# A linear-attention and gated-MLP block: a smaller mask build, other start-up loads, numerators at a 64-column stride and a new written-out order

## The chip, the cores and the metric

The kernel runs on one core of one Trainium2 chip. The core has five engines that run side by side, each with its own queue of instructions: TensorE (PE, matmuls, with its weight loads shown apart as PEld), VectorE (DVE), ScalarE (ACT), GpSimd (POOL) and SyncE (SP, which here only issues DMAs). They wait for each other by semaphores. Each engine executes in the order of its queue, so an instruction that waits holds up all that is queued behind it on that engine.

The metric is the device time of one execution in microseconds, as a median of several executions. The kernel before takes 272.32 us (three executions, 272.31 to 272.6).

## The reference

One transformer block, on 2048 rows of 640 columns in bf16. The attention is linear: 32 heads of 20 columns, with a feature map of two softmaxes.

```python
qkv = x_normed @ wqkv                        # q, k, v: 32 heads of 20
pq, pk = q @ w_phi[h], k @ w_phi[h]          # per head, 20 x 20
phi_q = concat(softmax(pq), softmax(-pq))    # 40 features per head; phi_k alike
kv  = phi_k^T v                              # per head, 40 x 20
z   = sum over rows of phi_k                 # per head, 40
o   = (phi_q kv) / (phi_q z + 1e-6)
h   = x + o @ wo                             # x_normed is layernorm(x)
h2  = h + ((n @ w_gate) * (n @ w_up)) @ w_down   # n is layernorm(h)
```

## The kernel before

The rows are cut in 16 tiles of 128 (t = 0 to 15), the 640 columns in 5 chunks of 128. Since q and k are used only behind w_phi, the kernel first multiplies the weights: Wk times the block-diagonal matrix of w_phi, and the same for Wq. After that each tile goes through these steps, which the code names by a letter and the tile:

- `x`: load; `L1s`, `L1a`: mean and variance on VectorE; `L1l`, `L1e`: reciprocal root by a logarithm and an exponential on ScalarE, for groups of tiles (`LNG`); `L1n`: minus mean times root, the shift that ScalarE needs to form the normalized row; `xn`: the normalized row; `xt`: its transpose, by a DMA, or on TensorE (tiles in `TPE`) with a copy out of PSUM, `xte`.
- `K`, `V`, `Q`: the three products, ten matmuls of about 320 columns each. For tiles 0 and 1 they are cut in five pieces of two (`TSPLIT`). `Ve` copies V out of PSUM; `Kx` and `Qx` take the exponentials of plus and minus, `Ks` and `Qs` the sums, `Kr`, `Ke`, `Qr`, `Qb`, `Qe` the reciprocals, and `Kn` and `Qn` multiply by them, on GpSimd. `KV`: eleven small matmuls, summed over the tiles in two PSUM banks. `qT`: the query features are transposed by a DMA.
- After all 16 `KV` the sums are masked to the heads (`KVe0`, `KVe1`). `N`: the numerators and denominators of a tile, eleven matmuls of 63 columns (three heads of 20 columns and a denominator). `dd`, `rd`, `o` on VectorE: denominator plus epsilon, reciprocal, product. `oT`: a DMA transposes `o`; `O`: the output product; `h`: the residual sum; `hc`: the centred row; `L2q`, `L2v`, `L2r`: the second variance; `hT`: a DMA transposes the row.
- `U`: gate and up products for blocks of 256 or 512 rows (`FB`), `g` and `u` multiply them, `D` is the down product, `y` adds it to the residual, `w` stores the tile. The last tile's D is cut in three pieces of columns (`LASTCUT`).

At the start stand, in addition: `warm`, products of zeros that keep TensorE busy until the loads are there (`NWARM`, `zero` makes their operand); `id0`, `id1`: the identity matrix for TensorE's transposes; `gl0`, `gla`, `glb`: a mask of heads, GL, by selects on GpSimd; `w5` loads w_phi and `Ph` multiplies it by the mask; `wk0` to `wk4` load Wk, `WT` transposes a chunk of it on TensorE, `WTe` copies it out, `F1` multiplies the chunk by the masked w_phi and `Fe1` copies the result. `wqt` and `F0`, `Fe0` do the same for Wq, later. So the path to the first product is: load of wk, WT, WTe, F1, Fe1, K; and beside it: load of x, L1s, L1a, L1l, L1e, xn, xt, xte, K. `K3` is the first product behind those of tiles 0 and 1.

The order is not the program's: every operation has an entry in the table `PLAN`, `name:key:alternative:banks`. The key is its place: `arrange` (L694) sorts all operations by it and gives each engine its queue. The alternative picks one of the engines that the operation allows (`alts`). The banks are its places in PSUM (eight banks of 2 KB per partition) or in a rotating buffer; whoever takes a place waits for the last user of the one before. So a wait for a free bank is decided by the table too. `emit` puts in the semaphores.

Of the kernel before, what the change touches and what calls it, by code (L numbers as in the profile page):

```python
# [8 lines left out]
ALU = mybir.AluOpType  # L9
# [23 lines left out]

NB = 11
# [17 lines left out]
id1:5.17 WT2:5.52::0 WTe2:6.139 WT0:5.958::1 WTe0:6.724 xt1:6.375::2 xt0:6.654::3 xte0:7.309 F1_2:6.933::4 WT1:7.252::6 WTe1:7.894:1 wk3:3.66 WT3:7.669::7
L1s2:6.426 Fe1_2:7.45 WTe3:8.289 xte1:8.697:1 F1_0:8.086::0 Fe1_0:8.603:1 wk4:4.14:1 WT4:8.405::3 WTe4:9.104:1 F1_1:8.822::4 Fe1_1:9.339 x3:4.62:1 x6:5.1
L1s3:9.512 L1a2:10.3 F1_3:9.141::6 Fe1_3:9.923 va1:5.414 L1a3:10.422 K0_0:9.46::0 L1s6:10.531 F1_4:9.731::2 Fe1_4:10.507:1 L1s7:11.319 wv0:5.58:1 V0_0:10.1::4
wv1:6.06 L1l2:11.091 x4:6.54 K0_1:10.371 K0_2:10.642 L1e2:11.417 L1s5:12.105 ekz:6.244 L1n2:11.697 V1_0:10.913::6 V1_1:11.184 L1n3:11.921 xn3:12.223:1:2
L1s4:12.893 L1a4:13.803 L1a7:13.912 K1_0:11.455::2 x12:7.02 wv2:7.5:1 K1_1:11.726 K0_3:11.997 wv4:7.98:1 L1a5:14.021 xn2:14.13::3 K1_2:12.268 K1_3:12.539
K1_4:12.81 V0_1:13.081 Kx1_0:13.28::0 Kx1_1:13.864 V1_2:13.352 wv3:8.46 wu1:8.94 L1a6:14.642 wg4:9.42 V0_2:13.623 V0_3:13.894 V0_4:14.165 wqt4:9.9 Ve0:14.635::0
V1_3:14.436 xt3:14.707::2 xte3:15.184:1 L1l4:15.219 L1e4:15.545 L1n5:15.825 K0_4:14.986 x8:11.21 Kx0_0:15.638::1 Kx0_1:16.222 Ks1:15.592::0 L1n4:16.049
V1_4:15.257 xt2:15.528::3 K3:15.807::4 Ve1:16.806::1 L1n7:16.985:1 L1n6:16.273 xn6:17.39:1:0 Kr1:18.195 V3:17.163::0 Ke1:18.486 Kn1:18.82 xn4:18.632:1:1
xn7:19.437:1:2 x10:11.69 wqt0:12.17 Ve3:20.242::2 xn5:17.16::3 xt5:17.785 rqz:21.133 xte2:17.672:1 L1s9:18.081 L1s11:18.867 Kx3_0:20.826::2 Kx3_1:21.41  # L60
Ks0:19.654::1 Kr0:21.994 K2:18.519::6 Kx2_0:22.14::3 Kx2_1:22.724 wqt2:19.096 Ke0:23.308 L1a9:21.047 V2:19.875::2 L1a11:21.157 L1s10:21.265 L1s8:22.052
L1a8:22.962 L1a10:23.072 L1l8:23.454 xt7:20.405 K5:21.231::0 Kx5_0:23.636::4 Ve2:23.18:1:3 xt4:21.715 L1e8:24.22 L1n10:24.5 V5:22.587::4 Ks3:23.912::2
Kx5_1:24.313 Ks5:25.305::3 L1n9:24.724 Ks2:26.698::0 x14:23.026 xn9:28.09::3 xt6:23.506 V7:23.943::6 Ve5:24.897::4 V4:25.299::2 L1n8:24.948 xn8:25.481:1:2
K4:26.655::0 Kn0:25.172 wqt3:24.816 Kr3:26.286 KV0:28.011::4,5 KV1:28.344 L1n11:28.602:1 L1s14:28.777 Ve7:26.432::5 Ke3:27.016 wqt1:26.125 xn10:27.162:1:1
Ve4:27.967::6 V6:28.677::6 Kr2:28.551 Kn3:27.485 Ke2:28.842 xn11:29.564::0 L1s12:30.076 Kx4_0:28.988::1 Kx4_1:29.572 Kn2:29.798 Kr5:30.156 Ve6:30.302::7
Ks4:30.863::1 xt8:27.436 xt9:28.745 L1s13:32.257 L1a13:33.166 K6:30.033::2 F0_1:31.389::0 xt11:30.189 K7:31.708::6 Fe0_1:31.906 wg2:31.5 wg3:31.98 L1a12:33.276
Kx6_0:32.49::0 KV2:33.064 KV3:33.397 Kr4:33.074 Kx6_1:33.22 Ke4:33.804 Kn4:34.138 F0_3:33.73::0 Fe0_3:34.247:1 Sz:36.451 L1a14:34.987 wu0:32.459 V8:34.049::2
# [151 lines left out]
def pool_c(n):  # L219
    return 0.183 + 0.0017 * n  # L220
# [692 lines left out]
```

## Time and profile before

| | |
|---|---|
| median of three executions | 272.32 us |
| profiled execution, its own time | 272.55 us |
| its span, first to last instruction | 270.8 us |
| PE busy | 266.0 us, 98% |
| DVE busy | 161.6 us, 60% |
| ACT busy | 123.8 us, 46% |
| POOL busy | 72.8 us, 27% |
| DMA | 27.76 MB, q1 47.3% of 16 engines, q10 1.6% |
| granted TensorE clock | 1.000 |

Busy time is the union of an engine's instructions; matmuls overlap each other, so the sum of the lengths shown is more than the time they take. The idle time in front of an instruction stands in square brackets with what ended it. The chain of waits follows the work back from the last instruction, each step to what released it. A load's time to landing counts from its issue. q1 is the queue of SP's DMAs, q10 that of ScalarE's.

### The profile page before, as it was taken

What the parts mean: (1) busy time and instruction counts of PE and PEld (TensorE: products, weight loads), DVE (VectorE), ACT (ScalarE), POOL (GpSimd) and SP (SyncE); (2) the same over time, 40 slices, a digit from 0 to 9 for tenths busy, and PEclk for the clock granted to TensorE, in tenths of its full rate; (3) what the DMA queues carried; (4) which work ended last, traced back from release to release, by engine and by line L of the source; (5) the groups of instructions that cost most, each with busy time, mean ns of one, the idle gap of its engine ahead of it and who ended that gap; (6) DMA issues with size and microseconds to landing.
All of it is one profiled execution on the core that took longest, in us unless ns stands there. A gap on an engine that the chain in (4) does not pass through costs nothing.

```text
span 270.8 us, 5184 instructions
## 1 busy us (share of the span) xinstructions
PE 266.0 (98%) x2103; PEld 177.1 (65%) x2103; DVE 161.6 (60%) x295; ACT 123.8 (46%) x304; POOL 72.8 (27%) x98
## 2 busy tenths in 40 slices
PE   7999999999999999999999999999999999999996
PEld 3877787777777689865656747775445457544774
DVE  4989999989689978887754434223123312424224
ACT  3999999788846667232254443003213510032000
POOL 8124989999942222331000000000000000000000
DMA  6997899967947989589347032041000000100003
GB/s 185 323 249 159 128 299 329 146 140 134 196 91 149 131 180 157 62 167 120 59 91 105 0 73 51 0 69 30 29 0 15 0 0 27 69 5 1 2 24 104
DMA packets 66600, 27.76 MB, mean 103 GB/s; under 512 B 57744, under 2 KB 65296, under 8 KB 66576
## 3 DMA queue, kind: packets, MB, share of 16 engines
q1 hardware_dynamic: 65120, 26.42, 47.3%
q10 hardware_dynamic: 1456, 1.01, 1.6%
q8 instruction: 16, 0.26, 0.4%
q14 instruction: 8, 0.07, 0.1%
HBM read 11.00 MB, written 2.62 MB: 50 GB/s over the span
## 4 chain that ended last, share of the span: by engine, by line
PE 90%; DVE 3%; DMA 3%; ACT 2%; POOL 1%; issue 0%; SPq 0%; DVEq 0%; POOLq 0%
PE ps L652 38%; PE ps L476 22%; PE ps L671 19%; PE ps L609 6%; PE ps L520 2%; DMA scratch<-ph 2%; PE ps L582 1%; DVE o L599 1%; PE ps L405 1%; DMA w<-in_A_w_phi_dram 1%; DVE sm L596 1%; ACT scratch L245 1%; POOL Phi L374 1%; DVE S L550 1%; ACT ph L545 0%; ACT ek L626 0%
## 5 line engine op out<-in xcount | busy, mean ns | idle before, releaser
L652 PE MATMUL ps<-xnT,Wgu 128*128 128x512 bf16 (+1 forms) x600 | 107.0, 336 | 0.0
L652 PEld LDWEIGHTS ps<-xnT,Wgu 128*128 128x128 bf16 x600 | 58.1, 98 | 43.4 <-DVE ev L660 0.4
L657 ACT ACTIVATE gt<-ps 128x512 bf16<-128x512 f32 (+1 forms) x60 | 29.0, 510 | 94.2 <-PE ps L652 90.4
L476 PE MATMUL ps<-Wp,xnT 128*128 128x320 bf16 (+1 forms) x480 | 68.8, 299 | 0.3 <-DVE o L599 0.2
L660 DVE TENSOR_TENSOR ev<-ps,gt 128x512 bf16<-128x512 f32 (+1 forms) x60 | 33.3, 580 | 41.7 <-PE ps L652 28.8
L476 PEld LDWEIGHTS ps<-Wp,xnT 128*128 128x128 bf16 x480 | 45.5, 97 | 18.3 <-DVE o L599 0.7
L671 PE MATMUL ps<-Wd,ev 128*128 128x320 bf16 (+2 forms) x396 | 53.3, 295 | 0.0
L671 PEld LDWEIGHTS ps<-Wd,ev 128*128 128x128 bf16 x396 | 38.1, 98 | 14.8
L512 POOL TENSOR_TENSOR ek<-ek,SR 128x1280 bf16<-128x1280 bf16 x16 | 37.5, 2357 | 4.0 <-ACT SR L497 3.9
L683 DVE SCALAR_TENSOR_TENSOR Wp<-ps,rs,x_all 128x640 bf16<-128x640 f32 (+3 forms) x18 | 14.4, 807 | 38.2 <-PE ps L671 38.1
L550 DVE TENSOR_REDUCE S<-ph 128x66 f32<-128x1320 bf16 x16 | 24.0, 1521 | 3.5 <-ACT ph L547 3.4
L630 POOL TENSOR_SCALAR ln<-mv 128x1 f32<-128x1 f32 x8 | 1.5, 190 | 89.3 <-ACT ek L626 88.9
L492 DVE TENSOR_REDUCE SR<-ek 128x64 f32<-128x1280 bf16 x16 | 23.3, 1478 | 1.2 <-ACT ek L488 1.0
L609 PE MATMUL ps<-Wo,Wp 128*128 128x320 bf16 x160 | 24.0, 299 | 0.0
L564 POOL TENSOR_TENSOR ph<-ph,RQ 128x660 bf16<-128x660 bf16 x16 | 20.8, 1306 | 10.2 <-ACT RQ L560 10.0
L545 ACT ACTIVATE ph<-ps 128x600 bf16<-128x600 f32 x32 | 21.2, 679 | 4.3 <-PE ps L476 3.6
L488 ACT ACTIVATE ek<-ps 128x640 bf16<-128x640 f32 x32 | 21.1, 701 | 0.5 <-PE ps L476 0.5
L609 PEld LDWEIGHTS ps<-Wo,Wp 128*128 128x128 bf16 x160 | 15.4, 98 | 6.7
L615 DVE SCALAR_TENSOR_TENSOR x_all<-ps,x_all 128x640 bf16<-128x640 f32 x16 | 13.1, 820 | 9.3 <-PE ps L609 9.2
L599 DVE TENSOR_TENSOR o<-ps,sm 128x720 bf16<-128x720 f32 x16 | 14.4, 903 | 1.3 <-DVE sm L596 0.5
L626 ACT ACTIVATE ek<-x_all,mv 128x640 bf16<-128x640 bf16 x16 | 13.1, 821 | 2.8 <-DVE x_all L615 2.8
L624 ACT ACTIVATE xn<-x_all,mv 128x640 bf16<-128x640 bf16 x10 | 8.2, 825 | 9.5 <-DVE x_all L615 9.5
(64 smaller groups left out, 166.3 us busy)
## 6 DMA issues: line engine op xcount, KB each, us to landing
out_dram<-Wp SPq DMA_DIRECT2D x15, 160.0 KB, 1.9
x_all<-in_A_x_dram SPq DMA_DIRECT2D x6, 320.0 KB, 6.1
Wgu<-in_B_w_up_dram SPq DMA_DIRECT2D x5, 384.0 KB, 6.4
Wgu<-in_B_w_gate_dram SPq DMA_DIRECT2D x5, 384.0 KB, 4.1
Wd<-in_B_w_down_dram SPq DMA_DIRECT2D x2, 480.0 KB, 6.8
Wd<-in_B_w_down_dram ACTq DMA_DIRECT2D x2, 480.0 KB, 4.5
ev<-in_A_wqkv_dram SPq DMA_DIRECT2D x5, 160.0 KB, 3.8
Wp<-in_A_wqkv_dram SPq DMA_DIRECT2D x5, 160.0 KB, 5.9
```

The lines of the kernel that those rows point to most:

```text
L476: ins = e.matmul(pb(b, hb)[:, 0:n1 - n0], lhsT=T["xnT"][:, NC - 1 - c, P * t:P * (t + 1)], rhs=T["Wp"][:, POS[kind], c, n0:n1], start=(c = ...
L488: G.op("act", "%sx%d_%d" % (nm, t, s), lambda e, s=s, b=b, ek=ek: e.activation(out=T["ek"][:, ek.slots[0], 0:2 * D].rearrange("p (b h s f) ...
L492: G.op("dve", "%ss%d" % (nm, t), lambda e, ek=ek, sr=sr: e.tensor_reduce(out=T["SR"][:, sr.slots[0], 0, :], in_=T["ek"][:, ek.slots[0], 0: ...
L512: G.op("pool", "Kn%d" % t, lambda e, eng, ek=ek, sr=sr: e.tensor_tensor(out=T["ek"][:, ek.slots[0], 0:2 * D].rearrange("p (h f) -> p h f", ...
L545: e.activation(out=v[:, 0:10].rearrange("p (b g) j f -> p b g j f", b=2), in_=pp(b, 0, 300).rearrange("p b (g j f) -> p b g j f", j=3, f=D ...
L550: G.op("dve", "Qs%d" % t, lambda e, t=t, ph=ph: e.tensor_reduce(out=T["S"][:, t, 0:66].rearrange("p (g k) -> p g k", k=6), in_=pv(ph).rear ...
L564: return e.tensor_tensor(out=v, in0=v, in1=T["RQ"][:, rq.slots[0], 1, 0:33].rearrange("p (g j) -> p g j", j=3).unsqueeze(3).to_broadcast([ ...
L609: ins = e.matmul(pb(b, hb)[:, 0:320], lhsT=T["oT"][:, oT.slots[0], c, :], rhs=T["Wo"][:, c, 320 * hb:320 * (hb + 1)], start=(c == 0), stop ...
L652: ins = e.matmul(pb(b)[:, 0:n], lhsT=T["Wgu"][:, gu, c, P * ft:P * (ft + 1)], rhs=T["xnT"][:, NC - 1 - c, o0:o0 + n], start=(c == 0), stop ...
L657: G.op("act", "g%d_%d" % (bi, ft), lambda e, pg=pg, gt=gt, n=n: e.activation(out=T["gt"][:, gt.slots[0], 0:n], in_=pb(pg)[:, 0:n], func=AF ...
L660: o_ = G.op("dve", "u%d_%d" % (bi, ft), lambda e, pu=pu, gt=gt, hh=hh, ft=ft, n=n: e.tensor_tensor(out=T["hh"][:, hh.slots[0], ft, 0:n], i ...
L671: ins = e.matmul(pb(b, hb)[:, 0:w], lhsT=T["hh"][:, hh.slots[0], ft, P * tt:P * (tt + 1)], rhs=T["Wd"][:, ft, c0 + w * hb:c0 + w * (hb + 1 ...
```

## The change

- The mask GL is laid out with nine columns for each of the five chunks (`GW`), so that two selects build it in place of ten. Each `Ph` reads the columns of its chunks from it.
- The zero products have 256 columns in place of 512, and there are 22 (eight, and `NFILL` = 14) in place of 10; the zero operand is half as wide. The table places some of them between the first transposes.
- `L1n` is made once for each group of tiles, on VectorE, with one instruction; before, once for each tile, on GpSimd or VectorE. The groups of `LNG` are nine in place of six.
- `xn` can run on GpSimd too. By the table it does for tiles 3, 4, 5, 8 and 9; on ScalarE for tile 6 (before: 3, 4, 6, 7, 8, 10), on VectorE for the rest.
- Each group of three heads of a numerator lies 64 PSUM columns behind the one before, in two neighbouring banks, in place of 18 heads in each of two banks. `dd`, `rd` and `o` handle 33 heads' places in place of 36.
- Tiles 0 and 1 alone are turned on TensorE (`TPE`); 2 and 3 go by a DMA like the others.
- The last tile's D is cut at 320 and 576 columns; before, at 320 and 512. The middle piece (320 to 576) is the last of the kernel.
- The whole table `PLAN` is new, so all queues and all banks have another order. At the start, in order of issue: on ScalarE's queue `x1`, `wk0`; on SP's `w5`, `x0`, `x3`, `wk1`, `wk4`, `wk3`, `wk2`, `x4`, `x6`, `wv1`, `wv0`, `x2`, `wv3`, `wv2`, `wv4`, `wqt0`, `xt3`, `wqt4`, `xt4`, `xt5`, `x8`. (Before: `w5` on ScalarE's; on SP's `x1`, `x0`, `wk2`, `wk0`, `x2`, `wk1`, `wk3`, `wk4`, `x3`, `x6`, `wv0`, `wv1`, `x4`, `x12`, `wv2`, `wv4`, `wv3`, `wu1`, `wg4`, `wqt4`, `x8`.) TensorE: 15 zero products, `WT0`, five, `F1_0`, two, `WT1`, `xt1`, `WT3`, `WT4`, `WT2`, `xt0`, `F1_1`, `F1_3`, `F1_2`, `F1_4`, `K0_0`, `K0_1`, `K0_2`, `K1_0` and so on to `V0_4`, then `K3`, `V3`, `V4`. ScalarE: `WTe0`, `L1l1`, `L1e1`, `L1l0`, `Fe1_0`, `L1e0`, `WTe1`, `xte1`, `L1l3`, `WTe2`, `L1e3`, `Fe1_1` to `Fe1_4`. GpSimd: `id0`, `id1`, `gl0`, `gla`, `eps`, `glb`, `Ph0`, `Ph2`, `Ph1`, then the fills without `phz`, which follows `Kn7`.
- In the middle TensorE's order is `KV15`, `Q7`, `N0`, `N1`, `Q11`, `N2`, `Q8`, `N3`, `Q14`, `O0`, `N9`, `O1`, `O2`, `N4`, `Q12`, `O3`, `Q15`, `N5`, `O9`, `N7`, `U` (before: `KV15`, `Q7`, `N1`, `N0`, `Q14`, `N3`, `Q11`, `Q8`, `N2`, `O1`, `N9`, `Q12`, `N5`, `O0`, `O3`, `N4`, `O2`, `Q15`, `O9`, `N7`, `U`). Five loads of gate and up weights stand close to each other on the SP queue shortly ahead of it, with transposes `qT` between them, and of the loads of Wd three (before: one) come after it, the last of them a little before the first `D`.

```diff
+GW = 9
-LNG = [[0], [1], [2, 3], [4, 5, 6, 7], [8, 9, 10, 11], [12, 13, 14, 15]]
-TPE = (0, 1, 2, 3)
+LNG = [[0], [1], [2], [3], [4, 5], [6, 7], [8, 9], [10, 11], [12, 13, 14, 15]]
+TPE = (0, 1)
-NWARM = 10
-LASTCUT = [(0, 320), (320, 512), (512, 640)]
+NFILL = 14
+LASTCUT = [(0, 320), (320, 576), (576, 640)]
...
-    for c in (0, 4, 1, 2, 3):
...
-        G.op("pool", "gla%d" % c, lambda e, n=n, o=o, base=base: e.affine_select(
-            out=T["GL"][:, o:o + n], in_=T["GL"][:, o:o + n], compare_op=ALU.is_ge, fill=0.0, base=base,
-            pattern=[[-DH, n]], channel_multiplier=1), 0.22, LP, [gl_b[c]], [gl_b[c]], k)
...
+    G.op("pool", "gla", lambda e: e.affine_select(
+        out=T["GL"][:, :, :], in_=T["GL"][:, :, :], compare_op=ALU.is_ge, fill=0.0, base=0, pattern=[[P - 6 * DH, NC], [-DH, GW]],
+        channel_multiplier=1), 0.24, LP, [gl_b], [gl_b], -97)
...
-            return e.matmul(o, lhsT=T["zero"][:, 0:P], rhs=T["zero"][:, :], start=True, stop=True)
...
+    for k in range(8, 8 + NFILL):
+        G.op("pe", "warm%d" % k, lambda e: e.matmul(pb(wm_b)[:, 0:256], lhsT=T["zero"][:, 0:P], rhs=T["zero"][:, :],
+             start=True, stop=True), 0.11, LT, [z_b], [wm_b], -89, before=[G.by["warm%d" % j] for j in range(k)])
...
-        for t in tl:
-            if t > 1:
-                G.op("pool", "L1n%d" % t, lambda e, eng, t=t: e.tensor_scalar(
-                    out=T["nb"][:, t:t + 1], in0=T["mv"][:, t, 0:1], scalar1=T["rs"][:, t:t + 1], scalar2=-1.0, op0=ALU.mult,
-                    op1=ALU.mult), 0.2, LP, [rs_b[t], mv_b[t]], [nb_b[t]], 10 * t - 25, alts=[("dve", 0.07, LD)])
+        if z > 2:
+            G.op("dve", "L1n%d" % a, lambda e, a=a, z=z: e.scalar_tensor_tensor(
+                out=T["nb"][:, a:z], in0=T["mv"][:, a:z, 0], scalar=-1.0, in1=T["rs"][:, a:z], op0=ALU.mult, op1=ALU.mult), 0.075, LD,
+                [rs_b[t] for t in tl] + [mv_b[t] for t in tl], [nb_b[t] for t in tl], 10 * a - 25)
...
-             alts=[] if t < 2 else [("act", act_c(640, True), LA)])
+             alts=[] if t < 2 else [("act", act_c(640, True), LA), ("pool", 1.15, LP)])
...
-                y, h0, h1 = g // 6, 3 * g, 3 * g + BH[g]
-                ins = e.matmul(pb(b, y)[:, 21 * (h0 - 18 * y):21 * (h1 - 18 * y)], lhsT=T["phT"][:, phT.slots[0], g, :],
+                y, h0, h1 = g // 8, 3 * g, 3 * g + BH[g]
+                ins = e.matmul(pb(b, y)[:, 64 * (g % 8):64 * (g % 8) + 21 * BH[g]], lhsT=T["phT"][:, phT.slots[0], g, :],
...
-            out=T["o"][:, o.slots[0], :].rearrange("p (b h d) -> p b h d", b=2, d=DH), in0=nv(b, 0, 20),
-            in1=smv(sm, 1).unsqueeze(3).to_broadcast([P, 2, 18, DH]), op=ALU.mult), dve_c(720, True), LD, [b, sm], [o], kk)
+            out=T["o"][:, o.slots[0], 0:33 * DH].rearrange("p (g j d) -> p g j d", j=3, d=DH), in0=nv(b, 0, 20),
+            in1=smv(sm, 1).unsqueeze(3).to_broadcast([P, NB, 3, DH]), op=ALU.mult), dve_c(660, True), LD, [b, sm], [o], kk)
```

More of the change, by code (lines that the diff above doesn't have):

```diff
@@ L52 @@
[L52 to L67, printed above, removed]
@@ new lines @@
+warm11:3.529 x1:0.78:1 warm12:3.748 warm13:3.966 warm14:4.185 L1s1:3.388 wk0:1.26 id0:0.78 id1:1.018 WT0:4.403::1 WTe0:5.159 warm15:4.961 gl0:1.262 gla:1.425
+warm16:5.179 warm17:5.398 warm18:5.616 warm19:5.817 L1a1:4.298 eps:1.635 L1l1:5.744 x0:1.26 L1s0:4.407 L1a0:5.317 L1e1:6.07 xn1:6.308::0 glb:1.728 L1l0:6.163
+Ph0:2.585 Ph2:3.179 x3:1.74:1 L1s3:6.838 Ph1:3.773 F1_0:5.926::2 Fe1_0:6.444:1 warm20:6.245 L1e0:7.027 xn0:7.625::1 warm21:6.355 L1a3:8.155 wk1:2.22 wk4:2.7:1
+WT1:6.641::0 WTe1:7.12:1 xt1:6.975::4 wk3:3.18 WT3:7.607::5 WTe3:8.264 xte1:7.705 WT4:7.886::6 L1l3:8.388 wk2:3.66:1 WT2:8.165::7 WTe2:8.642 WTe4:8.672:1
@@ L270, in build_graph @@
     w5_b, phi_b = Buf("w5"), [Buf("phi%d" % k) for k in range(3)]
-    id_b, gl_b, eps_b = Buf("ident"), [Buf("gl%d" % c) for c in range(NC)], Buf("eps")
+    id_b, gl_b, eps_b = Buf("ident"), Buf("gl"), Buf("eps")
     mk_b = Buf("mask")
```

205 lines of the change are left out of this document (108 added, 97 removed).

## The prediction

> **What bounds the kernel now.** I read the page first, then the chain of waits, the timeline of TensorE, the other engines' timelines at the start, the waits, and the end.
>
> ```profile
> PE 266.0 (98%) x2103; PEld 177.1 (65%) x2103; DVE 161.6 (60%) x295; ACT 123.8 (46%) x304; POOL 72.8 (27%) x98
> PE 90%; DVE 3%; DMA 3%; ACT 2%; POOL 1%; issue 0%; SPq 0%; DVEq 0%; POOLq 0%
> ```
>
> TensorE is the bound and carries 90% of the chain. Its matmuls already follow each other closely (ten of 320 columns take 1.36 us in the chain), and the change leaves their sum almost alone. So only three things can move the time: how soon the products start, gaps between them, and the tail. First the start (TensorE's timeline, then the other engines'):
>
> ```profile
> 1.25 4.45 PE L365 MATMUL ps<-ev 128*128 128x512 bf16 x10 [1.25 <-DVE ev L360]
> 6.03 1.17 PE L386 MATMUL ps<-ident,ev 128*128 128x128 bf16 x10 [0.33 <-POOL ident L327]
> 7.04 0.72 PE L456 MATMUL ps<-ident,xn 128*128 128x128 bf16 x10
> ...
> 16.57 7.63 PE L476 MATMUL ps<-Wp,xnT 128*128 128x320 bf16 x55
> ```
> ```profile
> 3.19 0.49 DVE L422 BATCH_NORM_STATS2 st<-x_all 128x6 f32<-128x320 bf16 x1 [2.00 <-DMA x_all<-in_A_x_dram]
> 4.59 0.50 DVE L422 BATCH_NORM_STATS2 st<-x_all 128x6 f32<-128x320 bf16 x1 [0.28 <-DMA x_all<-in_A_x_dram]
> 5.60 0.29 POOL L327 TENSOR_SCALAR_AFFINE_SELECT ident<-ident 128x128 bf16<-128x128 bf16 x1
> 6.76 1.30 ACT L245 ACTIVATE scratch<-ps 128x640 bf16<-128x640 bf16 x2 [0.47 <-PE ps L386]
> 9.11 2.62 ACT L245 ACTIVATE Wp<-ps 128x640 bf16<-128x640 f32 x4
> ```
>
> The first turn of a weight (WT2) starts at 6.03: not for its weight, whose load landed 3.56 us after its issue at 1.72, at 5.28, but for the identity, made on GpSimd behind the mask. The row of 16.57 begins with K3, the first product after the start-up; I count the start by it. Then the middle, and the rows that free its PSUM:
>
> ```profile
> 79.12 3.16 PE L476 MATMUL ps<-Wp,xnT 128*128 128x300 bf16 x20
> 83.81 0.50 PE L582 MATMUL ps<-KVm,scratch 128*128 128x63 bf16 x11
> 84.50 1.54 PE L476 MATMUL ps<-Wp,xnT 128*128 128x300 bf16 x10 [0.20 <-DVE o L599]
> 92.00 1.52 PE L609 MATMUL ps<-Wo,Wp 128*128 128x320 bf16 x10
> 93.89 0.51 PE L582 MATMUL ps<-KVm,scratch 128*128 128x63 bf16 x11 [0.38 <-ACT ph L547]
> ```
> ```profile
> L599 DVE TENSOR_TENSOR o<-ps,sm 128x720 bf16<-128x720 f32 x16 | 14.4, 903 | 1.3 <-DVE sm L596 0.5
> L596 DVE RECIPROCAL sm<-sm 128x36 f32<-128x36 f32 x16 | 6.0, 377 | 0.4
> ```
>
> Starts less work give the losses: the 20 matmuls of 79.12 hold 0.25 (Q8 waits for bank space freed by an `o`), 83.81 to 84.50 is 0.69 for eleven of 0.34, so 0.35 (Q12, again `o`), and 92.00 to 93.89 is 1.89 for ten of 1.36, so 0.53 (N7 waits for Qx12, which waited for a transpose, qT7, landing after 5.3 us where its sixteen have a median of 3.7). Together 1.13 us. From 98 us on the chain is TensorE without a break. The end:
>
> ```profile
> 267.38 1.42 DVE L683 SCALAR_TENSOR_TENSOR Wp<-ps,rs,x_all 128x640 bf16<-128x640 f32 x2 [1.52 <-PE ps L671]
> 265.03 4.13 SPq L685 DMA_DIRECT2D out_dram<-Wp  x5
> ```
>
> The profiled execution took 272.55 (span 270.8 and 1.75 around it), 0.23 above the median of 272.32; the sum is made against 272.55 and 0.23 then taken off.
>
> **The start, part by part.** *Mask and identity.* Ten selects (196 and 194 ns) become two of 45 elements, 0.2 each, and id0, id1 (0.20 and 0.29) move ahead of them; the fill of `ph` (0.30 and 0.54) moves far back. The identity is ready near 1.4 instead of 5.89. What is late next is the weight. *Loads.* x1 and wk0 go to ScalarE's queue, w5 and the rest to SP's, in order of use. wk0 is second on its queue, issued near 1.28. Nearest rows: x0, second on SP's queue, landed 4.57; the next 160 KB load landed 5.28. I take 4.9, between them, for WT0; ends 4.57 and 5.67 (the fourth load, issued 2.19 and 3.5 us under way).
>
> The Trainium skill (DMA: Bandwidth & Descriptors, "Issuing engines are not separate DMA queues") says that DMAs of all issuing engines run on the same 16 DMA engines and interleave. By it the second queue saves nothing and wk0 lands as the third load, at 5.28: the start below comes 0.38 later and the sum is -0.3 instead of -0.7. The trace has no two large loads on two queues at this point.
>
> *From WT0 to K3.* ScalarE now carries nine of the twelve copies and folds out of PSUM, and its order sets K3. WT2's copy began 0.73 after WT2 (6.03, 6.76); ScalarE's copies start 0.59 apart (7.94, 8.53). After WTe0 come L1l1, L1e1, L1l0 (0.59, 0.33, 0.14), Fe1_0 at 1.4 to 1.7, L1e0, WTe1, xte1, L1l3, WTe2, L1e3 and four folds at 0.59: the third fold, Fe1_2, starts 5.0 after WTe0 and ends 0.7 later. K0_2 waits for it, at 0.73+5.75 = 6.5 after WT0; then 18 pieces of two matmuls at 0.272 are 4.9, so K3 stands 11.4 to 11.5 after WT0: 16.35, **-0.2**. The ends of wk0 give -0.5 and +0.6. The ln and exp pairs grow from six to nine (+3 x 0.5 on ScalarE); one pair, 0.46, is in this chain and counted.
>
> *Zero products.* Ten of 512 (0.427 apart) become 22 of 256, 0.213 each by half: 15 end at 4.45, before WT0; five (1.07) lie under WTe0's 0.73+0.70, two under L1e1 and its x row. Nothing, unless that cover goes: then 0.2 each.
>
> *Two tiles turned on TensorE.* Tiles 2 and 3 leave it: ten transposes of 0.056, 0.56 before K3, are in the count above by not being there. Two DVE copies (0.49 each) go; two DMA transposes come, 1.2 of SP's time each, 2.8 to landing. xt3 must land before K3: x row 3 on GpSimd begins about 10.3, 1.2 long, 1.25 issue, landing by 14.5 to 15.3, under the pieces of K and V. Loads behind it on SP wait for that row too: wqt4 and x8, whose users are some 4 us away.
>
> *Shifts per group.* Fourteen one-column rows (0.27 on GpSimd, 0.20 on DVE) become seven on DVE, about 0.2 each: +1.0 on DVE, 60% busy, beside TensorE's work. *Rows on GpSimd.* ScalarE loses five of 0.92, GpSimd gains five. Unseen there: 0.19 (its one-column row) to 1.31 (its two-input row of 660); I take 1.2. Three fall in its idle 7 to 17 us; two between 20 and 72 us, where it is busy 45.7 of 52, with `ph`'s fill (0.84) and less seven shift rows (1.9): net +1.4 against 6.3 idle. KV15 stood 0.81 behind the last Kn (74.21, 75.02). Nothing; if the cover goes, up to +0.5.
>
> **The middle.** At 64-column stride `o` has 660 elements and the reciprocal 33: 0.84 and 0.35, so 0.09 less per tile on DVE between a numerator and its freed banks. The waits on `o` come after three and four tiles: 0.27 and 0.36 earlier against 0.25 and 0.35. I take **-0.6** for both and leave the third, which hangs on a transpose. The order is new everywhere, so the ends are -1.1 (all gone) and 0 (other waits of that size in their place). Weight loads moved to 64 to 69 us stand between transposes on SP, but each needed tile has over 7 us of products before its numerator. The last Wd load (480 KB, 3.9 on ScalarE's queue when quiet) now comes some 5 us before the first down product: covered by about 1.
>
> **The tail.** The early last-tile piece shrinks from 128 to 64 columns, 12 x 0.027 = -0.32; the last piece grows from 192 to 256: +0.32, its DVE row +0.07, its store (64 KB between rows of 1.5 and 1.6) +0.03. **+0.1.**
>
> Sum: -0.2 - 0.6 + 0.1 = -0.7: 271.85 for a profiled execution, 271.6 against the median.
>
> **Rivals.** *A: the gaps only move.* For it: the new order frees banks as tightly as the old (Q14 behind Qx11, O1 behind `o3`, Q12 behind h1). The middle gives 0, the sum is -0.1: 272.2. Or the middle gives 0.6 and the queue nothing (wk0 at 5.28 to 5.67): -0.3 to 0.1, 272.0 to 272.4. Together 0.27: no change that can be told.
>
> *B: TensorE stays at half speed one period longer (slower).* Until 6.94 WT's matmuls start 0.107 apart, from 7.04 0.056; the granted clock reads 1.00 throughout, so only the spacing tells. The new fillers stop at 4.45 and resume after WT0, with a pause like the old one. If the step comes 3 us later, the work between WT0 and K0_2 (four turns, two x turns, five folds: 3.3 at full speed) takes 6.6 and the fillers 1.5, 8.1 in place of 6.5: +1.6 on the sum, 273.2. It decides from a delay of about 1.3 us. Against: the busy share of the first 7 us is as before. 0.09. The Trainium skill (TensorE: Matmul & The Clock Gate, "Part 1: The HAM clock gate") has the array at half clock until about 3.4 us of sustained activity, in a free-running window; that is this mechanism, and the step at 7.0 fits a window that began after the first product.
>
> *C: a late transpose (slower).* qT7's excess of 1.6 cost 0.53 because the rest was covered. The queue now holds 30+16+16 turned tiles instead of 28+16+16, and in the crowded stretch after N0 the turned `o` of tiles 0 to 3 have one or two products of cover. The same excess there, uncovered, costs up to 1.6: 273.2; it decides where less than 0.4 of it is covered. 0.12.
>
> *D: all goes well:* -0.5, -1.1, +0.1: 270.8. Chance 0.06.
>
> **Numbers.** The forecast, 271.6, gets 0.46 (own range 271.0 to 271.78). Less than 0.2%, 0.54 us, I count as no change: about what a measurement of this kernel can tell. Faster 0.46+0.06 = 0.52, same 0.27, slower 0.09+0.12 = 0.21. The range, 270.9 to 272.9, takes in A and the nearer halves of B, C and D.
>
> **What would show it.** Identity select before 2 us; WT0 at 4.6 to 5.3; the spacing step near 7; K3 near 16.35; no wait on `o` among the first Q and N; `o` near 0.84; last row some 0.5 long. Wrong if K3 is later than 17, if gaps above 0.3 stand between 75 and 100, or if GpSimd's x rows pass 1.8 and KV14 waits.

## The result and the profile after

The changed kernel takes **276.94 us** (median of four executions, 276.36 to 277.5) beside 272.44 (272.31 to 272.6) for the kernel before, measured with it: a ratio of 1.0165, interval 1.0138 to 1.0191. It is slower by 4.5 us; the forecast was 271.6. The profiled execution took 277.35 (span 275.6), 4.80 more than that of before.

Two lines of the page of the changed kernel, the busy time of each engine and the chain of waits by engine:

```profile
PE 265.4 (96%) x2090; PEld 178.0 (65%) x2105; DVE 158.1 (57%) x299; ACT 124.1 (45%) x309; POOL 80.5 (29%) x78
PE 77%; DMA 8%; DVE 8%; ACT 3%; POOL 2%; SPq 1%; issue 1%; DVEq 0%
```

TensorE's work is what it was (265.4 after 266.0; 15 of its 2105 matmul records are missing), but its share of the chain fell from 90% to 77%. DMA, VectorE and GpSimd have taken the difference. The groups of instructions of the changed kernel (busy us, mean ns of one, idle time before them and what ended it) say which matmuls waited and which row is new:

```profile
L474 PE MATMUL ps<-Wp,xnT 128*128 128x320 bf16 (+1 forms) x480 | 68.7, 299 | 3.9 <-DMA xnT<-xn 3.7
L445 POOL TENSOR_SCALAR xn<-x_all,mv,rs 128x640 bf16<-128x640 bf16 x5 | 12.5, 2502 | 8.6 <-DVE nb L435 8.6
L600 DVE TENSOR_TENSOR o<-ps,sm 128x660 bf16<-128x660 f32 x16 | 13.5, 845 | 0.7
```

K, V and Q now stand idle 3.7 us for turned rows (xnT). A row on GpSimd takes 2.50 us, where I had taken 1.2 with 1.31 as the upper end. The `o` row came out as forecast (0.84). The timeline of TensorE in the changed kernel shows where the idle time lies:

```profile
20.89 7.01 PE L474 MATMUL ps<-Wp,xnT 128*128 128x320 bf16 x50 [0.43 <-DMA xnT<-xn]
28.02 0.80 PE L404 MATMUL ps<-Phi,scratch 128*128 128x140 bf16 x12
28.66 0.83 PE L518 MATMUL ps<-ev,ek 128*128 128x63 bf16 x22
32.53 2.89 PE L474 MATMUL ps<-Wp,xnT 128*128 128x320 bf16 x20 [3.04 <-DMA xnT<-xn]
```

I count a wait by the spacing of the starts less the work of the matmuls between, as in the prediction. The wait at 32.53 (V6) is 3.20 so counted, that at 20.89 (K5) 0.60. By stretches the waits of before and after are 0.27 and 4.73 us from 17 to 50, 0.15 and 0.49 from 50 to 73, 1.67 and 1.76 from 73 to 98; ahead of 17 us they differ by 0.1. So nearly all of the loss lies in 33 us of K and V. SP's queue ahead of V6, in its timeline of the changed kernel (start, time of issuing, what, and how many):

```profile
15.86 3.62 SPq L463 DMA_TRANSPOSE xnT<-xn  x2
19.52 0.58 SPq L281 DMA_DIRECT2D x_all<-in_A_x_dram  x1
20.15 1.21 SPq L463 DMA_TRANSPOSE xnT<-xn  x1
21.40 0.57 SPq L281 DMA_DIRECT2D x_all<-in_A_x_dram  x1
22.02 3.97 SPq L305 DMA_TRANSPOSE scratch<-in_A_wqkv_dram  x3
26.03 0.58 SPq L281 DMA_DIRECT2D x_all<-in_A_x_dram  x1
26.66 5.85 SPq L463 DMA_TRANSPOSE xnT<-xn  x3
```

Two rows (tiles 4 and 5) follow each other on GpSimd, the second ending at 18.24. Only then can SP issue xt5 (18.27, the second transpose of the first line). Behind it SP issues x8, xt2, x10, three turned pieces of wqt and x14 without a pause, so xt6 is issued at 26.66, though its row was ready on ScalarE at 22.09. It lands 5.83 us later. VectorE is late by the same queue: L1s8 waits until x8 is there. The rows on GpSimd as its timeline shows them in the changed kernel:

```profile
10.36 2.50 POOL L445 TENSOR_SCALAR xn<-x_all,mv,rs 128x640 bf16<-128x640 bf16 x1 [3.49 <-DVE nb L435]
13.20 2.50 POOL L445 TENSOR_SCALAR xn<-x_all,mv,rs 128x640 bf16<-128x640 bf16 x1 [0.33 <-DVE nb L435]
15.64 0.13 POOL L349 MEMSET mask<- 128x33 bf16 x1
15.74 2.50 POOL L445 TENSOR_SCALAR xn<-x_all,mv,rs 128x640 bf16<-128x640 bf16 x1
```

V6's 3.20 us are two things: the late issue and a slow landing. In a second trace of the same order (the kernel with extra rows far behind, described below, which is the changed kernel up to 178 us) xt6 is issued at 26.70 and lands in 4.1 us. There V6 waits 0.79, K7 0.73 and K10 1.53:

```profile
30.88 1.53 PE L474 MATMUL ps<-Wp,xnT 128*128 128x320 bf16 x10 [0.63 <-DMA xnT<-xn]
32.97 1.53 PE L474 MATMUL ps<-Wp,xnT 128*128 128x320 bf16 x10 [0.56 <-DMA xnT<-xn]
...
59.05 1.53 PE L474 MATMUL ps<-Wp,xnT 128*128 128x320 bf16 x10 [1.36 <-DMA xnT<-xn]
```

The waits for turned rows add up to 4.5 us in the one trace and to 4.1 in the other, but they stand at other products. The lateness takes away the cover, and which transpose then lands too late differs from one execution to the next.

The start and the tail did what was forecast. In the timeline of the changed kernel (one row each of GpSimd, TensorE and, at the end, VectorE):

```profile
1.24 0.29 POOL L329 TENSOR_SCALAR_AFFINE_SELECT ident<-ident 128x128 bf16<-128x128 bf16 x1 [0.24 <-POOL ident L326]
...
4.78 0.72 PE L385 MATMUL ps<-ident,ev 128*128 128x128 bf16 x5 [0.28 <-DMA ev<-in_A_wqkv_dram]
...
273.01 0.48 DVE L684 SCALAR_TENSOR_TENSOR Wp<-ps,rs,x_all 128x256 bf16<-128x256 f32 x1 [0.43 <-PE ps L672]
```

The identity is there at 1.53, WT0 starts at 4.78 with its weight, K3 at 16.21 (16.57 before), and the last row takes 0.48.

### The profile page after: what moved, and what is told of

Same layout as the page of the kernel before. It is cut to its first block, busy times and chain, and to the rows that moved or that the text cites. A ratio compares the mean times of both kernels' runs of the same rounds, so it can differ in the third digit from the quotient of the medians.

```text
span 275.6 us, 5180 instructions
## 1 busy us (share of the span) xinstructions
PE 265.4 (96%) x2090; PEld 178.0 (65%) x2105; DVE 158.1 (57%) x299; ACT 124.1 (45%) x309; POOL 80.5 (29%) x78
## 4 chain that ended last, share of the span: by engine, by line
PE 77%; DMA 8%; DVE 8%; ACT 3%; POOL 2%; SPq 1%; issue 1%; DVEq 0%
PE ps L653 37%; PE ps L672 19%; PE ps L474 11%; PE ps L610 6%; DMA xnT<-xn 4%; POOL xn L445 2%; DMA scratch<-ph 2%; DVE o L600 2%; DVE SR L490 2%; DMA ev<-in_A_wqkv_dram 1%; PE ps L518 1%; DMA x_all<-in_A_x_dram 1%; PE ps L580 1%; SPq L463 1%; DVE xn L445 1%
## 5 line engine op out<-in xcount | busy, mean ns | idle before, releaser
L658 ACT ACTIVATE gt<-ps 128x512 bf16<-128x512 f32 (+1 forms) x60 | 29.6, 510 | 103.2 <-PE ps L653 93.5
L672 PE MATMUL ps<-Wd,ev 128*128 128x320 bf16 (+2 forms) x396 | 54.0, 295 | 0.0
L672 PEld LDWEIGHTS ps<-Wd,ev 128*128 128x128 bf16 x396 | 38.1, 98 | 15.3
L684 DVE SCALAR_TENSOR_TENSOR Wp<-ps,rs,x_all 128x640 bf16<-128x640 f32 (+3 forms) x18 | 14.5, 809 | 44.1 <-PE ps L672 44.1
L631 POOL TENSOR_SCALAR ln<-mv 128x1 f32<-128x1 f32 x4 | 0.8, 192 | 93.9 <-ACT ek L627 93.9
L610 PEld LDWEIGHTS ps<-Wo,Wp 128*128 128x128 bf16 x160 | 15.3, 98 | 7.6 <-issue 1.2
L445 POOL TENSOR_SCALAR xn<-x_all,mv,rs 128x640 bf16<-128x640 bf16 x5 | 12.5, 2502 | 8.6 <-DVE nb L435 8.6
L600 DVE TENSOR_TENSOR o<-ps,sm 128x660 bf16<-128x660 f32 x16 | 13.5, 845 | 0.7
```

What stands on the lines that cost most here:

```text
L610: ins = e.matmul(pb(b, hb)[:, 0:320], lhsT=T["oT"][:, oT.slots[0], c, :], rhs=T["Wo"][:, c, 320 * hb:320 * (hb + 1)], start=(c == 0), stop ...
L658: G.op("act", "g%d_%d" % (bi, ft), lambda e, pg=pg, gt=gt, n=n: e.activation(out=T["gt"][:, gt.slots[0], 0:n], in_=pb(pg)[:, 0:n], func=AF ...
L672: ins = e.matmul(pb(b, hb)[:, 0:w], lhsT=T["hh"][:, hh.slots[0], ft, P * tt:P * (tt + 1)], rhs=T["Wd"][:, ft, c0 + w * hb:c0 + w * (hb + 1 ...
```

## The experiments

The theory after the result: the rows on GpSimd are twice as long as I took them, and SP's queue carries their lateness to every transpose and load behind. Rivals: the new order of loads and transposes is late by itself; or the shifts made per group, or the numerators' stride, cost something. Each ratio is against the kernel before, measured in the same session, and gains in us are taken from the ratios. Line numbers are those of each kernel.

### Taking the rows off GpSimd

The third field of an entry in the table picks the engine (2 is GpSimd, 1 ScalarE, none VectorE); nothing else is touched.

```diff
-xn3:9.772:2:2
+xn3:9.772::2
-xn4:12.722:2:3
+xn4:12.722::3
-xn5:13.882:2:0
+xn5:13.882::0
...
-xn9:25.203:2:0
+xn9:25.203::0
-xn8:31.739:2:1
+xn8:31.739::1
```

> The changed kernel with its five GpSimd rows (tiles 3, 4, 5, 8, 9) moved to VectorE at the same places of the order; nothing else differs. Theory 1 (the row takes 2.50 us on GpSimd where 1.2 was assumed; xt5 waits for row 5 on SP's queue, and what is behind it comes 3 us late): the waits at K5 (0.6), V6 (3.2), F0_3 (0.3), K11 (0.4) and K10 (0.3) go, 272.2 us, 271.5 to 272.8. Theory 2 (the new order of loads and transposes on SP's queue makes xt6 late by itself, whoever makes the rows): V6 still waits 2 us or more, 274.5 to 276. Theory 3 (VectorE is too full for five more rows of 0.6): V6 does not wait, but other waits of 1 us or more come between 10 and 45 us, 273 to 274.

Measured: 273.98 us (273.67 to 274.47), 1.0054 (1.0034 to 1.0074). So 3.0 of the 4.5 us come from the engine of these rows, with the order of everything else kept; the rest of the loss isn't theirs, and the time stays above the 272.8 that was the upper end expected. xt6 is issued at 24.57, 2.1 earlier, and lands in 3.8; V6 and K5 wait no longer. Two waits for turned rows are left in TensorE's timeline of this kernel, K7 and K10 (0.85 and 0.75 by the spacing):

```profile
30.66 1.53 PE L474 MATMUL ps<-Wp,xnT 128*128 128x320 bf16 x10 [0.69 <-DMA xnT<-xn]
...
55.18 1.53 PE L474 MATMUL ps<-Wp,xnT 128*128 128x320 bf16 x10 [0.59 <-DMA xnT<-xn]
```

With tiles 8 and 9 on ScalarE instead of VectorE:

```diff
-xn9:25.203::0
+xn9:25.203:1:0
-xn8:31.739::1
+xn8:31.739:1:1
```

> The same with rows 3, 4, 5 on VectorE and 8, 9 on ScalarE. Theory 1: 272.2 us, 271.5 to 272.8, the waits at K5 and V6 gone. Theory 2: V6 still waits 2 us or more, 274.5 to 276. Theory 3: faster than with all five on VectorE by over 0.5 us.

Measured: 275.18 (274.7 to 275.33), 1.0094 (1.0071 to 1.0117). ScalarE is the worse place by about 1.1: KV0 waits 0.83 and K6 0.62 in this kernel, neither of which waits with the rows on VectorE.

### Which of the five rows

Row 5 alone on VectorE, since SP's long wait stands at its transpose:

```diff
-xn5:13.882:2:0
+xn5:13.882::0
```

> The changed kernel with row 5 alone on VectorE; rows 3, 4, 8, 9 stay on GpSimd. Theory 1, if SP's queue behind xt5 is the way of the loss: the waits at K5 and V6 go, 3.5 us of the loss, 273.0 us, 272.3 to 273.8. If instead GpSimd's total of 6.5 us more (its products Kn coming late) is the way: the waits stay but for some 0.7 us, 275.5 to 276.5. Theory 2: unchanged, 276 to 277.5.

Measured: 276.45 (275.58 to 276.83), 1.0139 (1.0114 to 1.0163). V6's wait is 0.78 here, but the time hardly moved: K3 waits 1.21 in this execution, K7 0.45, K10 1.02. xt3 is issued at 12.98 and lands at 17.46, after 4.5 us; in the changed kernel's trace it was issued at 12.89 and landed after 2.8. So K3's wait doesn't come from the row that was moved: xt3 stands behind row 3, which is on GpSimd in both kernels, and in the changed kernel's trace it had luck.

Rows 8 and 9 on VectorE, 3 to 5 on GpSimd:

```diff
-xn9:25.203:2:0
+xn9:25.203::0
-xn8:31.739:2:1
+xn8:31.739::1
```

> The changed kernel with rows 8 and 9 on VectorE and rows 3, 4 and 5 still on GpSimd. Rows 3 to 5 together and 8 and 9 together share the 3.0 us that all five cost. If the start-up rows (xt5 and what stands behind it on SP's queue) are most of it: 276.0 us, 275.3 to 276.7, V6 still waits 2 us or more. If the later two are most of it, by the products Kn that stand behind them: 274.3, 273.7 to 275.0.

Measured: 276.72 (275.57 to 277.47), 1.015 (1.0122 to 1.0178), the time of the changed kernel within its scatter. Taking the two later rows off GpSimd alone gives nothing back, so the loss of 3.0 needs the three rows of the start-up. That they make all of it is argued: a kernel with these three on VectorE and 8 and 9 left on GpSimd wasn't measured. The wait was not where I looked for it, either: V6 doesn't wait here, though xt6 is issued at 27.10, later than in the changed kernel; it lands in 3.7. K3 1.39, K7 1.54, F0_3 0.92 and K10 0.92 wait instead.

### The rows on GpSimd in the kernel before

The other direction: the old order, in which the same five rows are put on GpSimd.

```diff
-xn3:12.223:1:2
+xn3:12.223:2:2
-xn4:18.632:1:1
+xn4:18.632:2:1
-xn5:17.16::3
+xn5:17.16:2:3
-xn9:28.09::3
+xn9:28.09:2:3
-xn8:25.481:1:2
+xn8:25.481:2:2
```

> The kernel before with rows 3, 4, 5, 8, 9 on GpSimd at their old places of the order, and nothing else changed. Theory 1: each row 2.50; row 5 ends near 20 in place of 18.5 and row 4 near 22.5 in place of 20.4, SP's queue behind them is late by 1.5 to 2, and TensorE waits 1 to 3 us between 15 and 40: 273.5 to 275.5. Theory 2: the rows as such cost nothing, 272.3 to 272.8.

Measured: 277.26 (276.41 to 278.58) against 272.49, 1.0177 (1.0143 to 1.0212). One edit of the change, put into the old kernel, costs as much as the whole change: 4.8 us, where I had expected 1 to 3. TensorE's timeline of this kernel:

```profile
22.35 6.97 PE L476 MATMUL ps<-Wp,xnT 128*128 128x320 bf16 x50 [0.23 <-DMA xnT<-xn]
...
31.04 2.89 PE L476 MATMUL ps<-Wp,xnT 128*128 128x320 bf16 x20 [1.05 <-DMA xnT<-xn]
...
37.87 0.85 PE L520 MATMUL ps<-ev,ek 128*128 128x63 bf16 x22 [2.07 <-POOL ek L512]
```

By the spacing these are 0.40, 1.21 and 2.24, together 3.85; its profiled execution (276.41, the fastest of the four) stands 3.86 above that of before. The last and largest is the cost on GpSimd itself: KV2 waits for a `Kn` queued behind rows. So in this order more than half of what the trace shows comes by GpSimd's own queue, and the rest by the transposes.

### What a row costs on GpSimd

Twelve extra rows on GpSimd between 178 and 203 us, where it has nothing else to do, written into buffers that are no longer read:

```diff
+        ("row", lambda e: e.tensor_scalar(out=pr(0), ..., scalar1=T["mv"][:, 0, 0:1],
+            scalar2=T["rs"][:, 0:1], op0=ALU.subtract, op1=ALU.mult)),
+        ("plain", ... the same, not reversed ...),
+        ("one", lambda e: e.tensor_scalar(out=pout(2), in0=T["x"][:, 0, :], scalar1=T["rs"][:, 0:1], scalar2=None, op0=ALU.mult)),
+        ("imm", lambda e: e.tensor_scalar(..., scalar1=0.5, scalar2=2.0, op0=ALU.subtract, op1=ALU.mult)),
+        ("two", lambda e: e.tensor_tensor(out=pout(4), in0=T["x"][:, 0, :], in1=T["x"][:, 1, :], op=ALU.mult)),
+        ("half", ... "plain" on 320 columns ...),
```

> The changed kernel with twelve more instructions on GpSimd from about 175 us, where it is idle; they write to a buffer that nothing reads any more and leave the result as it is. Each of 640 columns, twice: the row as it stands (reversed chunks, two column scalars), the same not reversed, one multiplication by one column scalar, two constants, a product of two tensors, and the row on 320 columns. Theory a (the second operation and its column scalar cost a pass of their own): the row 2.5, one multiplication about 1.3, the constants 2.5. Theory b (the reversed writing costs): not reversed 1.3. Theory c (it is the time of a two-input row plus the scalars): product of two 1.27, half of the columns 1.3. The time of the whole stays 276.4 to 277.5.

Measured, in GpSimd's timeline of this kernel (rows in the order of the edit; the second round of six gave the same within 0.01, and the starts follow each other at these lengths within 0.04):

```profile
178.72 2.50 POOL L696 TENSOR_SCALAR ph<-x_all,mv,rs 128x640 bf16<-128x640 bf16 x1
181.22 2.50 POOL L698 TENSOR_SCALAR ph<-x_all,mv,rs 128x640 bf16<-128x640 bf16 x1
183.70 1.89 POOL L700 TENSOR_SCALAR ph<-x_all,rs 128x640 bf16<-128x640 bf16 x1
185.56 2.36 POOL L701 TENSOR_SCALAR ph<-x_all 128x640 bf16<-128x640 bf16 x1
187.88 1.39 POOL L702 TENSOR_TENSOR ph<-x_all 128x640 bf16<-128x640 bf16 x1
189.26 1.43 POOL L703 TENSOR_SCALAR ph<-x_all,mv,rs 128x320 bf16<-128x320 bf16 x1
```

The product of two tensors, whose like I had taken as the upper end, is the cheapest of the forms on 640 columns. One tensor with a scalar costs 1.89, with two operations 2.36 to 2.50. The reversed order of the chunks costs nothing, columns in place of constants 0.14. From 320 to 640 columns the row grows by 1.07: about 3.3 ns a column and 0.36 fixed. It takes 2.50 here, on a quiet GpSimd, as in the crowded start-up, so the length is the row's own and not due to neighbours. The kernel's one execution took 278.23, above the 276.4 to 277.5 expected; from one execution I draw nothing.

### The loads

What is left with the rows on VectorE: xt7 is issued behind x14, xt10 behind three loads of gate and up weights (384 KB each). First I set x14 behind xt7, and wg3, wg1 and wu4 behind xt10:

```diff
-x14:22.832
+x14:24.7
-wg3:44.483
+wg3:47.8
-wg1:44.963
+wg1:48.2
-wu4:47.102
+wu4:48.5
```

> The changed kernel with its five rows on VectorE (the run before: 273.98), and four loads on SP's queue set back: x14 from before xt6 to behind xt7, and three weight loads of 384 KB (wg3, wg1, wu4) from before xt12 and xt10 to behind xt10. Theory 2 in its smaller form (what is left of the loss is transposes that land late behind loads of the new order): the waits at K7 (0.85) and K10 (0.75) go, 272.4 us, 271.9 to 273.0. Rival (the transposes are slow by themselves): both waits stay, 273.7 to 274.3. If x14 was due where it stood, VectorE waits for it and a new wait of about 1 us comes near 30.

Measured: 274.77 (273.97 to 275.36), 1.0081 (1.0051 to 1.0111): not better. The waits of K7 and K10 are gone (0.10 of waits from 50 to 73 us in place of 0.86), but now VectorE stands 1.29 for x14, and F0_4, K9, K11 and O9 wait 0.68, 0.35, 0.81 and 0.99. So x14 goes forward instead, ahead of xt2:

```diff
-x14:24.7
+x14:16.9
```

> The changed kernel with its rows on VectorE (273.98), the three weight loads behind xt10 as in the run before, and x14 this time brought forward, to before xt2, in place of set back. Theory 2 in its smaller form: no wait at K10, none of over 0.3 at V6 and K7, VectorE does not wait for x14, 272.4 us, 271.9 to 273.0. Rival: the bytes ahead of xt2 to xt7 are the same, so the wait only moves, to K2 or F0_3 or stays at K7: 273.0 to 274.0.

Measured: 273.65 (272.91 to 274.12, nine executions), 1.0039 (1.0025 to 1.0054). The waits of K7 and K10 are gone. The interval overlaps that of the kernel without the moved loads, so by the time alone the gain of 0.4 isn't shown; by the trace two waits went (1.6) and K11's (0.97) came. The cause of K11's stands in the timelines of VectorE, GpSimd and TensorE of this kernel:

```profile
36.39 1.90 DVE L435 SCALAR_TENSOR_TENSOR nb<-mv,rs 128x2 f32<-128x2 f32 x1
...
40.82 0.15 DVE L435 SCALAR_TENSOR_TENSOR nb<-mv,rs 128x4 f32<-128x4 f32 x1
...
33.60 6.98 POOL L510 TENSOR_TENSOR ek<-ek,SR 128x1280 bf16<-128x1280 bf16 x3 [0.78 <-ACT SR L495]
...
41.57 4.67 PE L474 MATMUL ps<-Wp,xnT 128*128 128x320 bf16 x33 [0.80 <-DMA xnT<-xn]
```

A shift of a group, two columns by two columns, takes 1.90 us, and the same on four columns 0.15. The long one ends at 38.29, and GpSimd's second product of the three (Kn5, 35.91 to 38.27) ends 0.02 before. In the changed kernel L1n12 (44.03 to 44.87) ends with Kn7 (44.85) in the same way. The short ones ran while GpSimd did nothing, filled memory, or (L1n6 in the changed kernel, 0.16) made a row out of one tensor. Behind the long one xn11 is late, and with it xt11 and K11.

### The shift's form

The same kernel; the shift now has one tensor input and a column of scalars. Of each group only the first tile gets one, since the row of tile 6 alone, on ScalarE, still reads a shift.

```diff
-            G.op("dve", "L1n%d" % a, lambda e, a=a, z=z: e.scalar_tensor_tensor(
-                out=T["nb"][:, a:z], in0=T["mv"][:, a:z, 0], scalar=-1.0, in1=T["rs"][:, a:z], op0=ALU.mult, op1=ALU.mult), 0.075, LD,
+            G.op("dve", "L1n%d" % a, lambda e, a=a: e.tensor_scalar(
+                out=T["nb"][:, a:a + 1], in0=T["mv"][:, a, 0:1], scalar1=T["rs"][:, a:a + 1], scalar2=-1.0, op0=ALU.mult, op1=ALU.mult),
+                0.075, LD,
```

> The kernel with the five rows on VectorE and the moved loads (273.65, 1.0039), with the shifts of the rows made on VectorE by an instruction that has one tensor and one column of scalars instead of two tensors; only the first tile of each group gets one, since xn6 is the only row left on ScalarE that reads a shift. In the kernel without this edit L1n10 took 1.89 us (36.39 to 38.28) and ended with GpSimd's Kn5 (35.91 to 38.27), and K11 waited 0.97 for the xt11 behind it. Theory (an instruction of VectorE with two inputs in SBUF stands until GpSimd's running two-input product ends): every L1n takes 0.15 to 0.25 also beside a Kn, K11's wait goes, 272.7 (272.3 to 273.1). In before L1n11 has one tensor input and took 0.205 beside Kn3. Rival (it is the place in VectorE's order, not the form): L1n10 still takes over 0.8 where a Kn runs, 273.6.

Measured: 272.70 (272.13 to 273.12, eleven executions), 1.0013 (1.0004 to 1.0022). In VectorE's, GpSimd's and TensorE's timelines of this kernel:

```profile
36.70 0.16 DVE L435 TENSOR_SCALAR nb<-mv,rs 128x1 f32<-128x1 f32 x1
...
33.93 6.98 POOL L511 TENSOR_TENSOR ek<-ek,SR 128x1280 bf16<-128x1280 bf16 x3 [0.97 <-ACT SR L496]
...
40.43 5.62 PE L475 MATMUL ps<-Wp,xnT 128*128 128x300 bf16 x40
```

The shift takes 0.16 in the midst of the same three products, none of the seven takes over 0.22, and K11 doesn't wait. The form was the cause of the long shift and of K11's wait, and it was worth 0.7 us (1.0039 to 1.0013, the intervals apart).

Of the 4.5 us, 4.1 are now taken back by three edits: rows 3.0, loads 0.4, shifts 0.7. These are steps in this order of edits, not shares of the changed kernel: how long a shift takes depends on where it falls against a `Kn`. What remains above the kernel before is 0.4. It has a counterpart in the trace, one wait of about 1 us between 89 and 97 (before: N7's 0.54): O9 in the changed kernel, behind the exponentials of tile 12, which start at 95.66 when qT7 has landed after 4.66; in the last kernel O3 instead, for oT3, landed 4.4 after its issue. Nine transposes of `ph`, `o` and the rows stand close to each other on SP there. A seventh buffer for `ph` would show whether the exponentials' wait can go; there is no room for it in SBUF, so there is no measurement. That this wait is the whole remainder is argued, not shown.

### The parts that were to gain, alone in the kernel before

Numerators at the 64-column stride (the two last pairs of the change's diff, `dd` and `rd` on 33 places), nothing else:

```diff
-                y, h0, h1 = g // 6, 3 * g, 3 * g + BH[g]
+                y, h0, h1 = g // 8, 3 * g, 3 * g + BH[g]
...
-            in1=smv(sm, 1).unsqueeze(3).to_broadcast([P, 2, 18, DH]), op=ALU.mult), dve_c(720, True), LD, [b, sm], [o], kk)
+            in1=smv(sm, 1).unsqueeze(3).to_broadcast([P, NB, 3, DH]), op=ALU.mult), dve_c(660, True), LD, [b, sm], [o], kk)
```

> The kernel before with the numerators at 64-column stride and 33 places, and nothing else. The prediction's step: the product o takes 0.84 in place of 0.90, the waits of Q8 and Q12 on it (0.25 and 0.35) go: 271.9 us, 271.6 to 272.2. Rival (the waits only move on to the transposes): 272.2 to 272.6.

Measured: 271.95 (271.73 to 273.01, ten executions), **0.9982 (0.9972 to 0.9993)**, the lowest median of this study. In TensorE's timeline of this kernel, to be held against the rows at 79.12, 84.50 and 93.89 of before:

```profile
79.14 3.08 PE L476 MATMUL ps<-Wp,xnT 128*128 128x300 bf16 x20
...
84.31 1.54 PE L476 MATMUL ps<-Wp,xnT 128*128 128x300 bf16 x10
...
93.38 0.51 PE L582 MATMUL ps<-KVm,scratch 128*128 128x63 bf16 x11
```

Q8's wait is 0.17 in place of 0.25, Q12's 0.21 in place of 0.35, N7's 0.215 in place of 0.54. N7 starts at 93.38 in place of 93.89. So the two waits on `o`, which the stride was to remove, gave 0.22 of this 0.54. The saving did not add up over three and four tiles as I had summed it, since VectorE waits for the next numerator in between: the `dd` ahead of Q8 starts at 79.31 before and at 79.33 here. The larger part, 0.32, is N7's, where the transpose qT7 landed in 4.8 us here and in 5.3 before. Whether the stride did that isn't shown: in the last kernel below, which has the stride too, qT7 takes 5.2 and N7 waits 0.60.

The start alone, that is the identity ahead of the mask and x12 set back behind x10:

```diff
-id0:2.34
+id0:0.79
-id1:5.17
+id1:0.8
-x12:7.02
+x12:11.95
```

> The kernel before with two things of the changed start alone: the identity made before the mask on GpSimd, and the 320 KB load x12 set back from before wv2 to behind x10. The prediction's step: the first weight transpose starts at 5.3 in place of 6.03 and K3 some 0.3 to 0.6 earlier: 272.0 us, 271.8 to 272.3. Rival (ScalarE's copies, not the identity, set K3): no change, 272.3 to 272.7.

Measured: 272.64 (271.78 to 273.99, ten executions), 1.0007 (0.9989 to 1.0025): no gain. WT2 starts at 5.47 in place of 6.03, but V0_0 then waits 1.06 for wv0, landed at 10.86, and K3 starts at 16.64. What is late next in the old order of loads is a load.

Both together, with x6 set behind wv1 as well:

```diff
-x6:5.1
+x6:6.3
```

> The kernel before with the numerators at 64-column stride (measured alone: 271.95), the identity before the mask, x12 set back behind x10 and, new, x6 (320 KB) set back behind wv1, since with the earlier identity V0_0 waited 1.06 for wv0. If the load of wv0 was what took the gain of the earlier identity: V0_0 waits less than 0.3, K3 starts near 16.0 in place of 16.57, 271.4 us, 271.0 to 271.8, faster than both kernels. Rival (the loads of the start land when the DMA engines have moved so many bytes, and another of them is late next): 271.8 to 272.2.

Measured: 272.26 (271.8 to 273.9, twelve executions), 0.9996 (0.9977 to 1.0015). K3 starts at 16.02, half a microsecond before the old kernel's, and K5 gives 0.45 of it back, waiting for its own turned row. It doesn't beat the stride alone. Its profiled execution (273.9) has a pause of 1.5 us near 184, where a `y` waited 4.33 for a store; that is one execution, and I draw nothing from it.

## Why the prediction was wrong

**The step that failed** is "Rows on GpSimd": "Unseen there: 0.19 (its one-column row) to 1.31 (its two-input row of 660); I take 1.2", priced at "Nothing; if the cover goes, up to +0.5". The row measured 2.50, outside the bounds I gave. The upper bound was taken from a product of two tensors; the measured rows turn that round (1.39 for the product against 1.89 to 2.50 for one tensor with scalars). Five rows are 12.5 us of GpSimd in place of 6. The price failed for a second reason: I looked for the cost on GpSimd's own work (KV14) and put three rows in its idle stretch of the start-up, and had for SP's queue one sentence, on row 3: "Loads behind it on SP wait for that row too: wqt4 and x8, whose users are some 4 us away". For rows 4 and 5 the queue was put at nothing. Behind xt5 stood seven entries ahead of xt6, and without its wait V6 would have started 2.7 us after xt6's issue, less than most of these transposes took to land (2.6 to 5.8, median 3.3). The rows cost 3.0 us in the new order and 4.8 in the old. Which product pays depends on how long each landing takes; that some product pays once the issue is late is what all the kernels with slow rows at the start show (276.45 to 277.26).

**"Shifts per group", "about 0.2 each"**: right for the median (0.15), wrong for those beside a `Kn` (0.84 in the changed kernel, up to 1.90 where the rows lay otherwise). A mean from other rows of the same engine said nothing about a wait for the neighbour's product. In the order with rows and loads moved it was worth 0.7. What it cost in the changed kernel itself is open: in its trace the shift ahead of xn11 took 0.11, and K11's 0.375 there stands behind a transpose that landed in 4.3. The Trainium skill (GPSIMD Engine Reference, "8. Key points") states that GpSimd shares its SBUF interfaces with VectorE, with contention for VectorE instructions that have two SBUF inputs. The traces agree with it where GpSimd's instruction has two inputs too (1.90 beside Kn5), and show no delay beside its one-input row (0.16).

**The start (-0.2)** was right: WT0 at 4.78 (forecast 4.9), K3 at 16.21 (16.35), the zero products covered. Its gain of 0.36 was gone at K5. My reading of the Trainium skill (DMA: Bandwidth & Descriptors, "Issuing engines are not separate DMA queues"), that the second queue saves nothing and wk0 lands at 5.28, didn't hold: it landed at 4.74, issued by the second queue at 1.30 in place of 2.19. I had left out half of the section, which says that starting DMAs on several engines does save the time it takes to start them; the trace agrees with that. That x0, issued at 1.32, landed at 4.53, so close to wk0, fits the interleaving that the section states, but no run here tests it. xt3 landed at 15.65, after the 14.5 to 15.3 forecast; in two experiments with slow rows K3 waited 1.2 to 1.4 for it, so this cover was thin.

**The middle (-0.6)**: alone, in the old order, the stride gave 0.43 (272.38 to 271.95), but that this is near the forecast is in good part luck. The waits on `o` gave 0.22 by the trace, and 0.32 came from the wait of N7, which the forecast had left out. In the new order the gaps moved, as rival A had it: Q14 0.25 and O9 1.10, 1.35 where before had 1.13. The sign that I named, a gap above 0.3 between 75 and 100, was there.

**The tail (+0.1)**: the last row took 0.48 as forecast. From the first U to the end the span grew by 0.2 (176.4 to 176.7).

**The rivals.** B did not come: WT0's five matmuls take 0.72 and WT1's, at 7.22, 0.44, so the step lies near 7 as before. C is the nearest to what happened, a late transpose without cover, but I had priced it at one transpose in the stretch after N0. The late ones lay in the first 50 us, and what made them late was an engine ahead of them, with landings of up to 5.8 us on top.

## What to carry to other kernels

Price a row that moves to another engine by a row of the same kind on that engine; where the trace has none, no other kind bounds it from above, and the range has to hold twice the guess. When a DMA waits for an engine, write down all that stands behind it on the same queue and when each is used: one late row costs there as often as there are entries without slack. One trace shows one choice of these entries, so a wait that is gone from a trace isn't yet a gain: the time over several executions decides. A part that gains alone (here the stride, -0.18%) is worth measuring by itself, and its waits one by one, before it goes into a new order.

## What the runs showed of the hardware

- On GpSimd one tensor with two scalar operations takes 2.36 to 2.50 us on 128x640 in bf16, with one operation 1.89, a product of two tensors 1.39; about 3.3 ns a column and 0.36 fixed for the first.
- A VectorE instruction with two inputs in SBUF, of 2 columns, that takes 0.15 alone ended with the GpSimd product of two tensors that ran beside it (38.29 and 38.27; 44.87 and 44.85), up to 1.90 long. With one tensor input it took 0.16 there.
- The fourteen DMA transposes of rows in the changed kernel landed in 2.6 to 5.8 us, median 3.3. xt10 took 5.2 there and with the rows on VectorE, behind three loads of 384 KB, and 3.7 to 4.1 in the three kernels where these loads came after it. xt6, behind one load of 320 KB, took anything from 3.7 to 5.8 in six kernels with the same order of the queue; why isn't known.
